# GpSimd's elementwise work handed to ScalarE and VectorE in a retention + two-MLP kernel, with a planner that knows of shared access

## The chip, the core and the metric

The kernel runs on one core of a Trainium2 chip. The metric is the device time of one execution in microseconds. Engines are named as the profile names them: PE (TensorE, matmuls; PEld its weight loads), DVE (VectorE), ACT (ScalarE), POOL (GpSimd), SP (SyncE, which issues the DMAs).

## The reference

Retention attention (scores times a decay mask, no softmax) gives 2304 tokens of 512 features. Two MLPs follow.

```python
scores = (q @ k^T) / sqrt(64); x = (scores * D) @ v        # 4 batches, 8 heads, 576 x 64
h = max(x @ w_in, 0);  x = (h * h) @ w_out                 # 512 -> 2048 -> 512
g = x @ w_gate;  out = (g * sigmoid(g) * (x @ w_val)) @ w_out2   # 512 -> 1536 -> 512
```

## The kernel before, in words

**Matmuls in three parts.** Every fp32 operand of the MLPs is split into a rounded high part, `hi`, a ScalarE copy, and a low part, `lo`, a VectorE subtraction (helper `split`, L283, and others like it). A product is then three matmuls: high x high, high x low, low x high (`three`, L200 to L202; in `o_piece` L1217 to L1219).

**The first MLP** works through five blocks of tokens. The first two multiply plainly. The last three, some 210 to 464 us, use seven products in place of eight on 2x2 blocks (`mlp1_s`, once for each of 8 pairs of feature blocks, so 24 times). This needs sums of quarters of x, T1 to T4 (`fetch_x1`: two on VectorE, two on GpSimd), and of the weights, S1 to S4 (GpSimd, L326). For each half, `finish` squares the activation on GpSimd (L852), rounds it on ScalarE and takes the low part on VectorE (L864). The weights of the second MLP are rounded to float32, split and stored meanwhile (`convert2_pair`, with four sums on GpSimd, L405).

**The second MLP** makes three passes of 768 tokens. A pass has 12 steps, one for each block of 128 features. Each step (`mlp2_gv`) runs seven products of six 384-column matmuls into two PSUM banks, MA and MB by turns; between them stand pieces of the output product (`o_piece`, three 256-column matmuls, L1217 to L1219). VectorE adds the products up: C11 (L1078, behind product 2), C22 (L1081, into the tile `m`, behind product 5), C12 (L1084, behind 6), and t1 and t2 (L1097, L1100, times the value half). ScalarE copies products out (L1069, `m` and `u`) and takes the sigmoid (L1090); VectorE multiplies it in (L1094). Product 7 goes into the bank that C22 frees, product 4 into the one that C11 frees.

Two steps make a pair. The activations of a pair give four sums (S3, S1, S2, S4: `act_sum`, GpSimd, L1156), and these and the four blocks themselves are split into operands (`operand`, tiles `at`). At the end of a pass a tail of output pieces runs (products P1 to P7 of the output). In it ScalarE and VectorE add up the passes' results (`sums_out`: copies L1258, additions from PSUM L1265) with two sums of 128x768 on GpSimd (`both`, L1271). In the same time the next pass's x is made: seven x parts (B11, B12 ... T4) are split into `xc`, and T1 to T4 are four subtractions of 128x768 on GpSimd (`fetch_x`, L967). A part's `xc` tile comes free when the last step of the pass before has used it.

**The order** on every engine is made by a planner (`Plan.emit`). Each operation has an engine, a duration in us, dependencies and a rank. The planner plays the program through: of the operations that can start first it takes the one with the lowest rank (the sums behind a product have -3, activations and operands -2, x parts 4 to 60, weight conversions 100 and more), emits it, and moves on. Each engine then runs its list in that order and waits in place. In the planner of before, engines don't disturb each other.

Of the kernel before, what the change touches and what calls it, by code (L numbers as in the profile page):

```python
# [64 lines left out]
class Op:  # L65


    __slots__ = ("eng", "us", "fn", "deps", "after", "rank", "kb", "n", "out", "left", "ready", "end", "fill")

    def __init__(self, eng, us, fn, deps, after, rank, kb):  # L70
        self.eng, self.us, self.fn, self.rank, self.kb = eng, us, fn, rank, kb
        self.deps, self.after = list(deps), list(after)
        self.out, self.left, self.ready, self.end, self.fill = [], 0, 0.0, None, None


class Plan:
# [10 lines left out]
    def __call__(self, eng, us, fn, deps=(), rank=0.0, kb=0, key=None, after=()):  # L87


        o = Op(eng, us, fn, deps, after, rank, kb)  # L90
        o.n = len(self.ops)
        self.ops.append(o)
        if key is not None:
            self.named[key] = o
        return o

    def emit(self):
# [10 lines left out]
        free, lanes, left = {}, 0.0, len(self.ops)  # L108
        while left:
# [48 lines left out]
def kernel(ctx: ExitStack, tc: tile.TileContext, units, qtab, tab, w1, w2, out):  # L158
# [75 lines left out]
    def round32(box, rank, apart=False):  # L234
# [36 lines left out]
        p4 = do("DVE", 1.34, d4, [p2, p3, o2], rank)  # L271
# [3 lines left out]
    def split(get, n, out, place, rank, deps, cols=None):  # L275
# [10 lines left out]
        return do("DVE", 0.16 + 0.53 * n / 512, lo, [h], rank)  # L286
# [26 lines left out]
    def convert_s(p, rank):  # L313
# [16 lines left out]
        x = do("POOL", 0.87, add(2, 3, 2, ALU.add), [ld], rank)  # L330
        x = do("POOL", 0.87, add(3, 0, 3, ALU.subtract), [x], rank)
        x = do("POOL", 0.87, add(0, 2, 0, ALU.subtract), [x], rank)
        x = do("POOL", 0.87, add(1, 1, 0, ALU.subtract), [x], rank)
# [14 lines left out]
    def convert2_pair(box, f, rank, plain, summed, steps):  # L348
# [38 lines left out]
        front = lambda: do("DVE", 0.69, lo(low, 0, n), [h, *low_free], rank)  # L387
        back = lambda: do("DVE", 0.43, lo(rest, n, 768), [h], rank)
# [13 lines left out]
        for o, x, y, op in steps:  # L402
            def add(o=o, x=x, y=y, op=op):
                w = st["fm"].rearrange("p (s n) -> p s n", s=4)
                nc.gpsimd.tensor_tensor(out=w[:, o], in0=w[:, x], in1=w[:, y], op=op)  # L405
            l = do("POOL", 0.87, add, [l if o != steps[0][0] else need[o], need[o]], rank)
        h = do("ACT", 1.03, hi2, [l], rank)
        l = do("DVE", 1.22, lo2, [h], rank)
# [98 lines left out]
    def att_prep(c, rank):  # L507
# [148 lines left out]
    def mlp1_act(j, f):  # L656
# [138 lines left out]
    def mlp1_s(j, p, pieces):  # L795
# [93 lines left out]
        r0 = do("ACT", act, relu("g0", hi_half), [c12], -2)  # L889
# [4 lines left out]
        c21 = name("s21", do("ACT", act, relu("g1", lo_half, "MA"), [N_op[j, p, 6]], -3))  # L894
        hlo_op[j, f1] = finish("g1", f1, lo_half, [c21, e1])
# [54 lines left out]
    def fetch_x(b, rank):  # L950
# [15 lines left out]
        def sub(o, a, c):  # L966
            return lambda: nc.gpsimd.tensor_tensor(out=at(o), in0=at(a), in1=at(c), op=ALU.subtract)  # L967
# [18 lines left out]
        parts_in_order(part, lambda *a, deps: do("POOL", 2.4, sub(*a), deps, min(rank, 4) if b else rank), ld)  # L986
# [60 lines left out]
    def mlp2_gv(s, pieces):  # L1047
# [77 lines left out]
        si1 = name("si1", do("DVE", dve, silu(0, lo_half), [sg], -2))  # L1125
# [13 lines left out]
        si2 = name("si2", do("DVE", dve, silu(1, hi_half), [sg], -2))  # L1139
        t2_ = name("t2", do("DVE", dve, t2, [si2, c22_], -2))  # L1140
# [10 lines left out]
    def act_sum(b, q, out, x, y, op, deps, rank=-2):  # L1151
        def go():
# [415 lines left out]
```

## Time and profile before

| | us |
|---|---|
| median of 3 runs (888.36 to 889.59) | 888.45 |
| the profiled execution | 887.93 |
| its span, first to last instruction | 886.1 |
| PE busy | 865.6 |
| DVE busy | 639.2 |
| ACT busy | 471.6 |
| POOL busy | 354.5 |

A matmul's end is modelled and overlaps the next one's start, so PE's pace is read from the distance of starts. An instruction on DVE that waits stands later in its timeline; what it waited for is in brackets, where the trace shows it.

### The profile page before, as it was taken

How to read it: one execution, taken by the hardware profiler on the slowest of the kernel's cores; microseconds unless marked ns; L12 is line 12 of the kernel's file. 1: busy time of each engine (PE TensorE's matmuls, PEld its weight loads, DVE VectorE, ACT ScalarE, POOL GpSimd, SP SyncE). 2: the span in 40 equal slices, each digit the busy share in tenths (PEclk: the TensorE clock that was granted, in tenths of full speed). 3: DMA queues.
4: the chain of work that ended last, by engine and by line, in shares of the span. 5: the costliest groups of instructions: out<-in, count | busy, mean ns of one | idle time of the engine just before them, and what ended most of it. 6: DMA issues, size and time to landing. Idle time of an engine off the chain costs nothing.

```text
span 886.1 us, 15973 instructions
## 1 busy us (share of the span) xinstructions
PE 865.6 (98%) x5995; PEld 809.3 (91%) x5995; DVE 639.2 (72%) x938; ACT 471.6 (53%) x898; POOL 354.5 (40%) x333
## 2 busy tenths in 40 slices
PE   9799999999999999999999999989999989999998
PEld 7688878999899899989999999989999989999998
DVE  4899895637878978897887878596555587555565
ACT  2767674347667667676564544463333354333353
POOL 4131205653646566556581434252122144221231
PEclk9999999999999999999999999999999999999999
DMA  9777868998989698879889998959777767775772
GB/s 359 259 272 269 313 218 258 398 375 282 367 285 352 245 344 315 289 238 341 319 311 323 301 417 317 348 196 330 273 254 259 266 206 259 262 276 214 260 261 74
DMA packets 113085, 254.84 MB, mean 288 GB/s; under 512 B 8560, under 2 KB 67696, under 8 KB 103664
## 3 DMA queue, kind: packets, MB, share of 16 engines
q1 hardware_dynamic: 113008, 253.82, 81.2%
q8 instruction: 47, 0.77, 0.3%
q14 instruction: 30, 0.25, 0.1%
HBM read 195.59 MB, written 58.20 MB: 286 GB/s over the span
## 4 chain that ended last, share of the span: by engine, by line
PE 76%; DVE 13%; issue 3%; DMA 3%; ACT 3%; POOL 2%; SPq 0%; ACTq 0%; POOLq 0%; DVEq 0%
PE gv L200 12%; PE gv L201 12%; PE gv L202 12%; PE acc L201 6%; PE acc L202 6%; PE acc L200 6%; DVE at L283 4%; PE acc L1219 3%; PE acc L1217 3%; PE acc L1218 3%; PE hps L200 3%; PE hps L202 2%; PE hps L201 2%; PE sc L528 1%; PE xs L568 1%
## 5 line engine op out<-in xcount | busy, mean ns | idle before, releaser
L200 PE MATMUL gv<-xc,w 128*128 128x384 f32 x504 | 171.6, 340 | 6.5 <-DVE m L1081 5.7
L201 PE MATMUL gv<-xc,w 128*128 128x384 f32 x504 | 170.3, 338 | 0.0
L202 PE MATMUL gv<-xc,w 128*128 128x384 f32 x504 | 170.0, 337 | 0.0
L201 PE MATMUL acc<-h,w 128*128 128x512 f32 (+1 forms) x320 | 117.8, 368 | 1.1 <-DVE h L679 0.8
L202 PE MATMUL acc<-h,w 128*128 128x512 f32 (+1 forms) x320 | 117.6, 368 | 0.2
L852 POOL TENSOR_TENSOR g<-g 128x256 f32<-128x256 f32 x96 | 86.8, 913 | 77.2 <-ACT g L848 76.5
L200 PE MATMUL acc<-h,w 128*128 128x512 f32 (+1 forms) x320 | 117.3, 367 | 0.0
L200 PEld LDWEIGHTS gv<-xc,w 128*128 128x128 f32 x504 | 94.9, 188 | 9.2 <-DVE m L1081 7.0
L201 PEld LDWEIGHTS gv<-xc,w 128*128 128x128 f32 x504 | 95.3, 189 | 0.2
L202 PEld LDWEIGHTS gv<-xc,w 128*128 128x128 f32 x504 | 95.0, 189 | 0.0
L1219 PE MATMUL acc<-w,at 128*128 128x256 f32 x288 | 81.6, 283 | 0.0
L1218 PE MATMUL acc<-w,at 128*128 128x256 f32 x288 | 81.3, 282 | 0.0
L1217 PE MATMUL acc<-w,at 128*128 128x256 f32 x288 | 81.2, 282 | 0.0
L1069 ACT COPY m<-gv 128x384 f32<-128x384 f32 x72 | 34.6, 481 | 83.1 <-PE gv L202 81.9
L1156 POOL TENSOR_TENSOR st<-g,rs 128x384 f32<-128x384 f32 x18 | 21.7, 1204 | 141.1 <-DVE rs L1100 141.1
L405 POOL TENSOR_TENSOR f<-f 128x256 f32<-128x256 f32 x72 | 66.2, 919 | 29.2 <-DVE cw L362 18.4
L202 PEld LDWEIGHTS acc<-h,w 128*128 128x128 f32 x320 | 60.1, 188 | 10.9 <-DVE w L283 1.0
L864 DVE TENSOR_TENSOR h<-g,h 128x256 fp32r<-128x256 f32 x96 | 62.6, 652 | 7.6 <-ACT h L860 7.5
L200 PE MATMUL gv<-xb,w 128*128 128x256 f32 x238 | 67.2, 282 | 0.8 <-ACT m L835 0.4
L201 PEld LDWEIGHTS acc<-h,w 128*128 128x128 f32 x320 | 60.1, 188 | 8.6 <-DVE h L679 1.3
L201 PE MATMUL gv<-xb,w 128*128 128x256 f32 x238 | 66.9, 281 | 0.1
L202 PE MATMUL gv<-xb,w 128*128 128x256 f32 x238 | 66.8, 281 | 0.0
(175 smaller groups left out, 2246.4 us busy)
## 6 DMA issues: line engine op xcount, KB each, us to landing
w<-wdS SPq DMA_DIRECT2D x36, 1024.0 KB, 5.6
raw<-w SPq DMA_DIRECT2D x34, 1024.0 KB, 7.3
w<-wdP SPq DMA_DIRECT2D x36, 768.0 KB, 7.0
w<-ws SPq DMA_DIRECT2D x94, 256.0 KB, 4.9
w<-wdOP SPq DMA_DIRECT2D x54, 256.0 KB, 4.8
w<-wdOS SPq DMA_DIRECT2D x18, 768.0 KB, 7.4
ws<-cw SPq DMA_DIRECT2D x16, 512.0 KB, 7.2
wdS<-cw SPq DMA_DIRECT2D x12, 512.0 KB, 5.3
```

The lines of the kernel that those rows point to most:

```text
L200: nc.tensor.matmul(ps, lhsT=wh, rhs=xh, start=first, stop=False, skip_group_check=onto)
L201: nc.tensor.matmul(ps, lhsT=wh, rhs=xl, start=False, stop=False, skip_group_check=onto)
L202: nc.tensor.matmul(ps, lhsT=wl, rhs=xh, start=False, stop=last, skip_group_check=onto)
L283: nc.vector.tensor_tensor(out=t[:, 1], in0=get(), in1=t[:, 0].bitcast(F32), op=ALU.subtract)
L405: nc.gpsimd.tensor_tensor(out=w[:, o], in0=w[:, x], in1=w[:, y], op=op)
L852: return lambda: nc.gpsimd.tensor_tensor(out=st[key][:, half], in0=st[key][:, half], in1=st[key][:, half], op=ALU.mult)
L864: nc.vector.tensor_tensor(out=t[:, 1, half], in0=st[key][:, half], in1=t[:, 0, half].bitcast(F32), op=ALU.subtract)
L1069: nc.scalar.copy(out=st[name], in_=late[bank][:, :HALF])
L1156: nc.gpsimd.tensor_tensor(out=o, in0=i, in1=k, op=op)
L1217: nc.tensor.matmul(ps, lhsT=ah, rhs=wh, start=product not in ONTO and q == 0 and off == 0, stop=False, skip_group_check=True)
L1218: nc.tensor.matmul(ps, lhsT=ah, rhs=wl, start=False, stop=False, skip_group_check=True)
L1219: nc.tensor.matmul(ps, lhsT=al, rhs=wh, start=False, stop=q == NQ - 1, skip_group_check=True)
```

## The change

Five groups of operations leave GpSimd: the 96 squares of the first MLP go to ScalarE (`Square`); the x subtractions of both MLPs (6 and 12), the two sums at each pass's end (6) and the sums of activations (72) go to VectorE. GpSimd keeps the attention's scalings and the sums of weights (L326, L405).

The planner gets a new rule. Operations with `lock=True`, and all of GpSimd's, run at a share of their speed while one of the other engine's runs beside them: VectorE at 0.5, GpSimd at 0.62. The durations that the planner is given are lowered to match. All orders are then made anew.

```diff
+SHARE = {"DVE": 0.5, "POOL": 0.62}
...
             free[o.eng] = t + o.us
+            if o.lock:
+                other = run.get("POOL" if o.eng == "DVE" else "DVE")
+                us = o.us
+                if other and other[0].end > t + 1e-9:
+                    x, since, both, left_x = other
+                    left_x -= max(0.0, min(t, both) - since) * SHARE[x.eng] + max(0.0, t - max(both, since))
+                    first = min(us / SHARE[o.eng], left_x / SHARE[x.eng])
+                    ends = [t + first + max(0.0, w - first * SHARE[e]) for w, e in ((us, o.eng), (left_x, x.eng))]
+                    grow(x, ends[1])
+                    run[x.eng] = x, t, t + first, left_x
+                    run[o.eng] = o, t, t + first, us
+                    free[o.eng] = ends[0]
+                else:
+                    run[o.eng] = o, t, t, us
...
-        p1 = do("DVE", 1.0 if apart else 0.8, d1, [o1], rank)
-        p2 = do("DVE", 1.0 if apart else 0.8, d2, [p1], rank)
-        p3 = do("DVE", 0.87, d3, [o2] if apart else [p2, o2], rank)
+        p1 = do("DVE", 0.69, d1, [o1], rank, lock=True)
+        p2 = do("DVE", 0.69, d2, [p1], rank, lock=True)
+        p3 = do("DVE", 0.75, d3, [o2] if apart else [p2, o2], rank, lock=True)
...
         def sub(o, a, c, deps):
-            eng, us = ("DVE", 0.69) if o in ("T1", "T2") else ("POOL", 1.5)
-            e = nc.vector if eng == "DVE" else nc.gpsimd
-            return do(eng, us, lambda: e.tensor_tensor(out=at(o), in0=at(a), in1=at(c), op=ALU.subtract), deps, rank)
+            eng, us = ("DVE", 0.69)
+            return do(eng, us, lambda: nc.vector.tensor_tensor(out=at(o), in0=at(a), in1=at(c), op=ALU.subtract), deps, rank, lock=True)
...
         def square(key, half):
-            return lambda: nc.gpsimd.tensor_tensor(out=st[key][:, half], in0=st[key][:, half], in1=st[key][:, half], op=ALU.mult)
+            return lambda: nc.scalar.activation(out=st[key][:, half], in_=st[key][:, half], func=ACTF.Square)
+
+        def gate(key, half, deps, bank=None):
+            r = do("ACT", act, relu(key, half, bank), deps, -3 if bank else -2)
+            return r, do("ACT", act, square(key, half), [r], -2)
...
-            r = do("POOL", 0.87, square(key, half), deps, -2)
-            h = do("ACT", act, hi, [r, y_op.get(order1[i - 2])], -2)
-            return do("DVE", 0.58, lo, [h], -2)
+            h = do("ACT", act, hi, [*deps, y_op.get(order1[i - 2])], -2)
+            return do("DVE", 0.42, lo, [h], -2, lock=True)
...
-        def sub(o, a, c):
-            return lambda: nc.gpsimd.tensor_tensor(out=at(o), in0=at(a), in1=at(c), op=ALU.subtract)
+        def sub(o, a, c, deps):
+            eng, us = ("DVE", 0.96)
+            return do(eng, us, lambda: nc.vector.tensor_tensor(out=at(o), in0=at(a), in1=at(c), op=ALU.subtract), deps, min(rank, 4) if b else rank, lock=True)
...
-            nc.gpsimd.tensor_tensor(out=o, in0=i, in1=k, op=op)
-
-        s_op[b, q, out] = do("POOL", 1.18, go, deps, rank)
+            e.tensor_tensor(out=o, in0=i, in1=k, op=op)
+
+        eng, us, e = ("DVE", 0.55, nc.vector) if out in ("S3","S1","S2","S4") else ("POOL", 1.02, nc.gpsimd)
+        s_op[b, q, out] = do(eng, us, go, deps, rank, lock=True)
...
-                nc.gpsimd.tensor_tensor(out=box(dst), in0=box(dst), in1=box(src), op=ALU.add)
-            c_op[b, name] = do("POOL", 2.9, go, deps, -3)
+                nc.vector.tensor_tensor(out=box(dst), in0=box(dst), in1=box(src), op=ALU.add)
+            c_op[b, name] = do("DVE", 0.96, go, deps, -3, lock=True)
```

What this does to the order: on PE every matmul keeps its place. VectorE has 96 instructions more, ScalarE 96 more, GpSimd 192 fewer. Lines of the changed kernel stand up to 27 lower in the file than the same ones of before.

VectorE, last step of pass 1, before: `rs<-gv` is C11, `m<-gv` is C22, `at` are operand splits and `xc` splits of the next pass's x.

```order
L1078 TENSOR_TENSOR rs<-gv_2049,m_6299 128x384
L283 TENSOR_TENSOR xc<-ys,xc 128x768
L283 TENSOR_TENSOR at<-st,at 128x384
L283 TENSOR_TENSOR at<-rs,at 128x384 x4
L1081 TENSOR_TENSOR m_6344<-gv_2048,m_6344 128x384
L1084 TENSOR_TENSOR rs<-gv_2049,u_6329 128x384
L1094 TENSOR_TENSOR rs<-rs,sg 128x384
L283 TENSOR_TENSOR xc<-ys,xc 128x768
```

The same place after the change:

```order
L1104 TENSOR_TENSOR rs<-gv_2049,m_6299 128x384
L305 TENSOR_TENSOR at<-st,at 128x384
L305 TENSOR_TENSOR at<-rs,at 128x384 x4
L1120 TENSOR_TENSOR rs<-rs,sg 128x384
L1107 TENSOR_TENSOR m_6346<-gv_2048,m_6346 128x384
L305 TENSOR_TENSOR xc<-ys,xc 128x768
L1110 TENSOR_TENSOR rs<-gv_2049,u_6328 128x384
L1123 TENSOR_TENSOR rs<-gv_2048,rs 128x384
L305 TENSOR_TENSOR xc<-ys,xc 128x768
```

Ahead of C22 the x split is gone (it follows C22), and the product with the sigmoid, `rs<-rs,sg`, has moved up.

VectorE, end of the tail of pass 1, before: `oc` from `gv_2050` and `hps` is the addition behind output product P6.

```order
L283 TENSOR_TENSOR xc<-ys,xc 128x768
L283 TENSOR_TENSOR at<-rs,at 128x384 x2
L283 TENSOR_TENSOR xc<-ys,xc 128x768
L283 TENSOR_TENSOR at<-rs,at 128x384
L283 TENSOR_TENSOR xc<-ys,xc 128x768
L283 TENSOR_TENSOR at<-rs,at 128x384 x2
L1265 TENSOR_TENSOR oc<-gv_2050,oc 128x512
L1265 TENSOR_TENSOR oc<-hps,oc 128x256
L283 TENSOR_TENSOR at<-rs,at 128x384
L283 TENSOR_TENSOR xc<-ys,xc 128x768
L283 TENSOR_TENSOR at<-rs,at 128x384
```

The same place after:

```order
L993 TENSOR_TENSOR ys<-ys 128x2x384
L305 TENSOR_TENSOR at<-rs,at 128x384 x2
L993 TENSOR_TENSOR ys<-ys 128x2x384
L305 TENSOR_TENSOR at<-rs,at 128x384
L1292 TENSOR_TENSOR oc<-gv_2050,oc 128x512
L1292 TENSOR_TENSOR oc<-hps,oc 128x256
L1298 TENSOR_TENSOR oc<-oc 128x768 x2
L1292 TENSOR_TENSOR oc<-acc_5444,oc 128x512
L1292 TENSOR_TENSOR oc<-hps,oc 128x256
L305 TENSOR_TENSOR at<-rs,at 128x384 x2
L305 TENSOR_TENSOR xc<-ys,xc 128x768 x2
L993 TENSOR_TENSOR ys<-ys 128x2x384
```

Between the splits stand three of the four subtractions (`ys<-ys`; the first is a few rows above), and the two pass-end sums (`oc<-oc`) follow the first addition, the second addition follows them; two x splits and the last subtraction come behind. In the next row C11 of pass 2 follows.

ScalarE, where the third of the first MLP's five blocks turns into the fourth, before: `g<-g` is the activation's Relu, `h<-g` its rounding, `m<-hps` a product copied out of PSUM, `f<-raw` a conversion of the second MLP's weights, `yt<-acc` the third block's result.

```order
L848 ACTIVATE g_3307<-g_3307 128x256
L848 ACTIVATE g_3253<-g_3253 128x256
L860 CAST h<-g_3253 128x256
L241 ACTIVATE f<-raw 128x1024
L919 COPY yt<-acc 128x512
L848 ACTIVATE g_3307<-gv_2048 128x256
L860 CAST h<-g_3253 128x256
L835 COPY m_3360<-hps 128x256
```

A like place after; here the second `g<-g` of a tile is its square:

```order
L869 ACTIVATE g_3247<-g_3247 128x256
L856 COPY m_3276<-gv_2049 128x256
L885 CAST h<-g_3175 128x256
L873 ACTIVATE g_3247<-g_3247 128x256
L400 CAST cw<-f 128x1024
L869 ACTIVATE g_3298<-g_3298 128x256
L873 ACTIVATE g_3298<-g_3298 128x256
L263 ACTIVATE f<-raw 128x1024
L885 CAST h<-g_3247 128x256
L869 ACTIVATE g_3298<-gv_2048 128x256
```

The squares stand in ScalarE's list between the Relu and the rounding.

## Rows read from the trace of the kernel before

**Rows 1.** The page, part 1: engine, busy us (share of the span), instructions.
```profile
PE 865.6 (98%) x5995; PEld 809.3 (91%) x5995; DVE 639.2 (72%) x938; ACT 471.6 (53%) x898; POOL 354.5 (40%) x333
```

**Rows 2.** Busy us by stretch: PE, PEld, DVE, ACT, POOL; granted clock; DMA share; GB/s.
```profile
200.00:460.00 260.00, 258.01 (x1680) 234.63 (x1679) 217.62 (x314) 175.28 (x369) 156.76 (x166) 1.00 0.87 306
```

**Rows 3.** Waits of PE in the whole span: us in total, times, longest.
```profile
PE gv L200 <- DVE m L1081: 5.7, 3, 2.8
PE hps L201 <- DVE x L600: 1.8, 1, 1.8
...
PE hps L1217 <- DVE oc L1265: 1.1, 2, 0.6
PE acc L201 <- DVE h L679: 0.8, 1, 0.8
...
PE gv L200 <- ACT m L835: 0.4, 1, 0.4
...
PE hps L200 <- DVE g L842: 0.2, 1, 0.2
```

**Rows 4.** Timeline of PE at the end of pass 1: start, us, engine, line, operation.
```profile
578.18 0.33 PE L201 MATMUL gv<-xc,w 128*128 128x384 f32 x1
578.36 0.34 PE L202 MATMUL gv<-xc,w 128*128 128x384 f32 x1
581.46 0.69 PE L200 MATMUL gv<-xc,w 128*128 128x384 f32 x1 [2.76 <-DVE m L1081]
581.94 0.52 PE L201 MATMUL gv<-xc,w 128*128 128x384 f32 x1
```

**Rows 5.** Busy us by stretch, columns as in Rows 2.
```profile
28.00:31.00 3.00, 1.63 (x7) 1.35 (x8) 2.45 (x3) 0.52 (x1) 0.15 (x1) 1.00 0.52 130
...
581.40:584.80 3.40, 3.35 (x13) 3.35 (x14) 2.36 (x4) 0.90 (x2) 0.00 (x0) 0.53 0.42 138
```

**Rows 6.** Timeline of DVE in the same place.
```profile
573.87 0.56 DVE L1078 TENSOR_TENSOR rs<-gv,m 128x384 f32<-128x384 f32 x1 [1.50 <-PE gv L202]
...
575.67 5.26 DVE L283 TENSOR_TENSOR at<-rs,at 128x384 fp32r<-128x384 f32 x4
580.85 0.55 DVE L1081 TENSOR_TENSOR m<-gv,m 128x384 f32<-128x384 f32 x1
581.32 0.54 DVE L1084 TENSOR_TENSOR rs<-gv,u 128x384 f32<-128x384 f32 x1
```

**Rows 7.** Timeline of POOL in the same place.
```profile
575.37 4.21 POOL L967 TENSOR_TENSOR ys<-ys 128x768 f32<-128x768 f32 x2 [2.13 <-DVE xc L283]
```

**Rows 8.** Groups by line and shape: count | busy us, mean ns | idle before.
```profile
L852 POOL TENSOR_TENSOR g<-g 128x256 f32<-128x256 f32 x96 | 86.8, 913 | 77.2 <-ACT g L848 76.5 <-DMA wdS<-f 0.3
...
L246 ACT ACTIVATE r<-raw 128x1024 int32<-128x1024 uint16 x34 | 39.0, 1148 | 0.0
...
L669 ACT ACTIVATE r<-r 128x256 f32<-128x256 f32 x16 | 6.7, 419 | 0.5
...
L733 DVE TENSOR_TENSOR xs<-xs 128x512 f32<-128x512 f32 x6 | 4.8, 807 | 0.1
```

**Rows 9.** Timeline of DVE in a quiet block of pass 2.
```profile
662.93 0.56 DVE L1100 TENSOR_TENSOR rs<-m,rs 128x384 f32<-128x384 f32 x1
665.44 0.56 DVE L1078 TENSOR_TENSOR g<-gv,m 128x384 f32<-128x384 f32 x1 [1.95 <-PE gv L202]
```

**Rows 10.** Timeline of DVE in the tail of pass 1.
```profile
586.68 0.55 DVE L1100 TENSOR_TENSOR rs<-m,rs 128x384 f32<-128x384 f32 x1
...
598.88 0.95 DVE L283 TENSOR_TENSOR xc<-ys,xc 128x768 fp32r<-128x768 f32 x1
599.74 0.55 DVE L283 TENSOR_TENSOR at<-rs,at 128x384 fp32r<-128x384 f32 x1
...
602.02 0.68 DVE L1265 TENSOR_TENSOR oc<-gv,oc 128x512 f32<-128x512 f32 x1
```

**Rows 11.** Timeline of PE, the first matmul of pass 2.
```profile
606.77 0.34 PE L200 MATMUL gv<-xc,w 128*128 128x384 f32 x1
```

More of the change, by code (lines that the diff above doesn't have):

```diff
@@ L65, with __init__ @@
 class Op:
-    __slots__ = ("eng", "us", "fn", "deps", "after", "rank", "kb", "n", "out", "left", "ready", "end", "fill")
-    def __init__(self, eng, us, fn, deps, after, rank, kb):
+    __slots__ = ("eng", "us", "fn", "deps", "after", "rank", "kb", "n", "out", "left", "ready", "end", "fill", "lock")
+    def __init__(self, eng, us, fn, deps, after, rank, kb, lock):
         self.eng, self.us, self.fn, self.rank, self.kb = eng, us, fn, rank, kb
         self.deps, self.after = list(deps), list(after)
-        self.out, self.left, self.ready, self.end, self.fill = [], 0, 0.0, None, None
+        self.out, self.left, self.ready, self.end, self.fill, self.lock = [], 0, 0.0, None, None, lock or eng == "POOL"
 class Plan:
@@ L85, in __init__, with __call__ @@
         self.ops, self.named = [], {}
-    def __call__(self, eng, us, fn, deps=(), rank=0.0, kb=0, key=None, after=()):
-        o = Op(eng, us, fn, deps, after, rank, kb)
+    def __call__(self, eng, us, fn, deps=(), rank=0.0, kb=0, key=None, after=(), lock=False):
+        o = Op(eng, us, fn, deps, after, rank, kb, lock)
         o.n = len(self.ops)
@@ L107, in emit, with grow @@
                 waiting.setdefault(o.eng, []).append(o)
-        free, lanes, left = {}, 0.0, len(self.ops)
+        free, lanes, left, run = {}, 0.0, len(self.ops), {}
+        def grow(o, end):
+            for x, whole in o.out:
+                if whole:
+                    x.ready = max(x.ready, x.ready if x.end else end + (0.0 if x.eng == o.eng else 0.08))
+            o.end = free[o.eng] = end
         while left:
@@ L132, in emit @@
             else:
-                o.end = t + o.us
+                o.end = free[o.eng]
             for x, whole in o.out:
@@ L270, in round32 @@
         converts.append(o1)
-        p4 = do("DVE", 1.34, d4, [p2, p3, o2], rank)
+        p4 = do("DVE", 1.24, d4, [p2, p3, o2], rank)
         r_users.append(p4)
@@ L329, in convert_s @@
         ld = do("SP", 0.4, load, [wf_saved[p], f_users[-2]], rank - 20, kb=512, after=raw_loads[-1:])
[L330 to L333, printed above, removed]
+        x = do("POOL", 0.75, add(2, 3, 2, ALU.add), [ld], rank)
+        x = do("POOL", 0.75, add(3, 0, 3, ALU.subtract), [x], rank)
+        x = do("POOL", 0.75, add(0, 2, 0, ALU.subtract), [x], rank)
+        x = do("POOL", 0.75, add(1, 1, 0, ALU.subtract), [x], rank)
         def store():
@@ L386, in convert2_pair @@
                     [("xbdone", NB - 1), ("ysv", NB - 2)] if home == "xs" else [("ysv", NB - 1)])
-        front = lambda: do("DVE", 0.69, lo(low, 0, n), [h, *low_free], rank)
-        back = lambda: do("DVE", 0.43, lo(rest, n, 768), [h], rank)
+        front = lambda: do("DVE", 0.69, lo(low, 0, n), [h, *low_free], rank, lock=True)
+        back = lambda: do("DVE", 0.43, lo(rest, n, 768), [h], rank, lock=True)
         if steps is GV_SUMS:
@@ L405, in add @@
                 nc.gpsimd.tensor_tensor(out=w[:, o], in0=w[:, x], in1=w[:, y], op=op)
[L406 removed]
+            l = do("POOL", 0.75, add, [l if o != steps[0][0] else need[o], need[o]], rank)
         h = do("ACT", 1.03, hi2, [l], rank)
[L408 removed]
+        l = do("DVE", 1.22, lo2, [h], rank, lock=True)
         e = w_dram[summed, f]
@@ L518, in att_prep @@
         if c not in FIRST:
-            qs_op[c] = do("POOL", 1.45, qs, [A_op[c], Q_op[c]], rank, after=[ks_op[c - 1]])
+            qs_op[c] = do("POOL", 1.27, qs, [A_op[c], Q_op[c]], rank, after=[ks_op[c - 1]])
         if c not in LAST:
-            ks_op[c] = do("POOL", 1.25, ks, [V_op[c], tab_op], rank, after=[qs_op[c]])
+            ks_op[c] = do("POOL", 1.04, ks, [V_op[c], tab_op], rank, after=[qs_op[c]])
     def att_scores(c, rank, fill=None):
@@ L893, in mlp1_s @@
         product(6, "MA", [c22])
-        c21 = name("s21", do("ACT", act, relu("g1", lo_half, "MA"), [N_op[j, p, 6]], -3))
-        hlo_op[j, f1] = finish("g1", f1, lo_half, [c21, e1])
+        c21, r1 = gate("g1", lo_half, [N_op[j, p, 6]], "MA")
+        name("s21", c21)
+        hlo_op[j, f1] = finish("g1", f1, lo_half, [r1, e1])
         y(take_y[3])
@@ L984, in part @@
             return l
-        parts_in_order(part, lambda *a, deps: do("POOL", 2.4, sub(*a), deps, min(rank, 4) if b else rank), ld)
+        parts_in_order(part, sub, ld)
         do.named["ysdone", b] = x_chain[-1]
@@ L1138, in mlp2_gv @@
         sg = do("ACT", act, sig(1, hi_half), [c12_, sg], -2)
-        si2 = name("si2", do("DVE", dve, silu(1, hi_half), [sg], -2))
-        t2_ = name("t2", do("DVE", dve, t2, [si2, c22_], -2))
+        si2 = name("si2", do("DVE", dve, silu(1, hi_half), [sg], -2, lock=True))
+        t2_ = name("t2", do("DVE", dve, t2, [si2, c22_], -2, lock=True))
         other(2)
```

12 lines of the change are left out of this document (6 added, 6 removed).

## The prediction

> **What bounds the kernel now.** I read first the page's engine line, then the waits of PE, then the stretch around the longest wait on each engine. PE is busy 865.6 of 886.1 us [rows 1]: 20.5 us is all that can be won, unless matmuls themselves slow down. The order shows every matmul at its old place, so only waits change.
>
> The table of waits tells whose they are [rows 3]. The largest entry is 5.7 us in three waits, two of about 2.8 us, where product 7 of a step waits for `m` (the sum C22, L1081). They lie in the last step of pass 1 and of pass 2. At pass 1's end the matmul before the gap starts at 578.36 and the next at 581.46, where its neighbours stand 0.18 apart [rows 4]. Behind the gap one lasts 0.52 instead of 0.33, and the granted clock of 581.4 to 584.8 is 0.53, nearly all of it at the 1.2 GHz level [rows 5]. So the price of one such place is 2.8 us of idleness and 3.4 x (1 - 0.53) = 1.6 us of slow matmuls: 4.4.
>
> VectorE's timeline says why C22 was late [rows 6]. Its instructions are 0.47 apart when nothing disturbs them (580.85 to 581.32), but the four operand splits that stand ahead of C22 take 5.26 us, 1.3 each. In just that time GpSimd runs two subtractions, 575.37 to 579.58 [rows 7]. I read this as two engines slowing each other on SBUF.
>
> **The change part by part.** The profiled execution took 887.93 us (886.1 of span and 1.8 around it), 0.5 under the median 888.45; I sum against 887.93.
>
> *x subtractions and the last step of a pass.* In the new order five splits and one product (`rs<-rs,sg`) stand ahead of C22, and no GpSimd instruction is left there. From the start of C11 at 573.87 the seven take 7 x 0.47 = 3.3, to 577.2. C22 also needs product 5, whose last matmul was six intervals before the one at 578.36, at 577.3, and lasts 0.34: 577.65. C22 then starts near 577.8, ends 0.56 later, and product 7, free at 578.36 + 0.18, waits 0 to 0.2. Both places: 2 x 4.4 = 8.8 us gone. Bounds: 0 if the splits stay slow, 9.0 at most.
>
> *What takes the place of the stall: the tail of a pass.* The subtractions, the pass-end sums and three sums of activations now stand among the splits on VectorE. From the last activation product of pass 1 to C11 of pass 2 the order has 14 splits and 3 sums of activations at 0.47, 3 x-splits, 4 subtractions and 2 pass-end sums of 768 elements at 0.86 (598.88 to 599.74), and four additions from PSUM, two at 0.60 (the 0.68 of the first less the 0.08 by which neighbours overlap) and two of half the size at an estimated 0.33 [rows 10]: 8.0 + 7.7 + 1.9 = 17.6 us. A subtraction is priced as an x-split, which reads two tensors of that size in SBUF. The time between those two points is some 22 us, from 586.68 [rows 10] to a C11 two products (12 x 0.175) behind 606.77 [rows 11]. But the first addition needs P6 of the last pair, 15 output pieces ahead of the pass's end. A piece is three matmuls of 256 columns at two thirds of 0.175 each, 0.35 us, so P6 is done 5.3 us before pass 2 begins. Behind it stand 0.9 + 1.7 + 0.9 + 0.9 + 1.7 + 0.9 = 7.0 us, up to C11 at +1.7; C11 is due at +2.2. The margin is half a microsecond, and 0.7 more before product 4 waits. I take 0 here, bounds 0 to 2 us a pass end. The wait of 1.1 us on `oc` (L1265) in these tails [rows 3] goes, since that addition no longer stands behind slowed splits: +1.1, bounds 0 and 1.1.
>
> *Sums of activations.* 72 leave GpSimd. On VectorE each costs about 0.47. In an odd step three of them come between the last product (662.93) and the next C11 (665.44), where VectorE is idle 1.95 us [rows 9]: 1.4 fits, with 0.5 left. Cost 0; if that cover failed by 0.2 in each of the 18 pairs, 3.6 us.
>
> *Squares.* 96 squares leave GpSimd (0.91 each) for ScalarE, where a square of 128x256 takes 0.419 [rows 8]: 40.2 us more. In the stretch of the three seven-product blocks ScalarE is busy 175.3 of 260 us [rows 2], so 215.5, or 83%. PE waited for it there 0.4 us in one entry [rows 3]. I cost it at 0; the cover is the slack of the copies of `m` and `u`, and its loss is the slow rival below. The activation's chain gets shorter: 0.42 on the engine that makes the next step anyway, in place of 0.91 and a hop.
>
> *First MLP's x subtractions.* Six more on VectorE at 0.81 [rows 8] is 4.9 us, beside 217.6 busy of 260 [rows 2]. GpSimd loses 96 squares there, which gives VectorE far more than it takes. Of the seven smaller waits behind the first 200 us, from 0.8 to 0.2 and 2.6 together [rows 3], I take half: +1.3, bounds -1 and 2.6.
>
> *First 200 us.* Nothing moves engine, but the planner's new costs reorder rounding on VectorE; PE waits there up to 1.8 at once [rows 3]. I take 0, bounds -3 and +2.
>
> *Sum.* 8.8 + 1.1 + 1.3 = 11.2 off, less 1.2 for new small waits (an estimate between 0 and the 3.6 above): 10 off. 887.93 - 10 = 877.9; I give 878.
>
> **Rivals.**
> - *VectorE becomes the tail's bound* (0.17). For it: the margin at C11 is half a microsecond. Each 0.1 us that the instructions of the last stretch or the chain behind P6 run over is then paid at two pass starts. A C11 or x-split that comes 2 us too late, twice, gives 4 us back: 882. If the clock falls as behind the 2.8 us gaps, it is 2 x (2 + 1.6) = 7, and 885, which I take as its price. In the trace the clock stayed at 1.00 around the wait of 1.8 us for `x` near 28 us [rows 3, 5], which speaks for the smaller figure. The Trainium skill (TensorE: Matmul & The Clock Gate, Part 1) calls the throttled state the default, which only activity releases; by it the new pauses would cost the clock too, and the larger figure would hold. Against the rival: 17.6 us of work stand in 22.
> - *The relief does not come* (0.08): splits are slow for another reason, such as waits for ScalarE's casts. Then C22 again starts at 573.9 + 0.5 + 5 x 1.3 + 0.5 = 581.4, and both stalls stay: 887 to 888, no change. Against it: GpSimd's two subtractions cover exactly the slow splits.
> - *ScalarE holds up PE in the first MLP* (0.15), the slower side. ScalarE runs in order, and a conversion's activation takes 1.15 us [rows 8]; at 83% a copy of `m` can find one ahead of it and a square too, 1.6 us. It decides once a copy ends later than one product and two output pieces after its own product, about 2 us. If each of 24 pairs loses 0.8 us, that is 19, and with the 10 won, 897. Against it: 0.4 us waited so far.
>
> **How the numbers follow.** My forecast has 0.60, and its own range is 874 to 882. The rivals have 0.17, 0.08 and 0.15. The range 873.5 to 889.5 takes in the first two and the beginning of the third; some 0.05 lies below and 0.12 above. Under 0.2% (1.8 us) this kernel can't tell a change from none. Faster is 0.60 + 0.17 = 0.77, the same 0.08, slower 0.15.
>
> **What would show it.** The waits of PE should have no entry of 2.8 us on C22, the granted clock should stay at 1.00 around the pass ends, and splits there should stand 0.47 apart. New waits of PE at the start of passes 2 and 3, on `xc` or C11, would show the first rival; waits on `m` or `u` copies from 200 to 460 us the third. I am wrong if the stalls at the pass ends stay, or if what PE gains there it loses in the first MLP.

## The result and the profile after

The changed kernel takes 876.25 us (median of 4 runs, 875.07 to 877.39), against 888.4 for the one before on the same chip (4 runs, 886.47 to 889.59): a ratio of 0.9865, 95% interval 0.9842 to 0.9888. The prediction was 878. The profiled execution took 875.07 us, the shortest of the four, with a span of 873.1, 13.0 shorter than before; by the medians it is 12.2.

The page's engine line after, columns as in [rows 1]:

```profile
PE 859.2 (98%) x5995; PEld 807.5 (92%) x5995; DVE 625.5 (72%) x1034; ACT 505.3 (58%) x994; POOL 132.3 (15%) x141
```

VectorE has 96 instructions more and is busy 13.7 us less: what it took over costs less than what it no longer waits for.

PE's waits after, columns as in [rows 3]:

```profile
PE hps L224 <- DVE w L305: 2.0, 1, 2.0
PE hps L223 <- DVE x L622: 1.6, 1, 1.6
PE spare L577 <- DVE P L559: 1.5, 1, 1.5
...
PE hps L584 <- POOL kv L533: 0.4, 1, 0.4
```

The 5.7 us on `m` that led [rows 3] have no successor. The three that lead now lie in the first 200 us. Behind 200 us three waits of 0.4 to 0.6 us are left, two of them in the last tail.

VectorE in the last step of pass 1, the place of [rows 6]:

```profile
569.72 0.56 DVE L1104 TENSOR_TENSOR rs<-gv,m 128x384 f32<-128x384 f32 x1 [0.91 <-PE gv L224]
570.19 0.55 DVE L305 TENSOR_TENSOR at<-st,at 128x384 fp32r<-128x384 f32 x1
570.66 1.96 DVE L305 TENSOR_TENSOR at<-rs,at 128x384 fp32r<-128x384 f32 x4
572.53 0.55 DVE L1120 TENSOR_TENSOR rs<-rs,sg 128x384 f32<-128x384 f32 x1
573.61 0.56 DVE L1107 TENSOR_TENSOR m<-gv,m 128x384 f32<-128x384 f32 x1 [0.52 <-ACT xc L301]
574.08 0.95 DVE L305 TENSOR_TENSOR xc<-ys,xc 128x768 fp32r<-128x768 f32 x1
```

The four splits take 1.96 us where they took 5.26. C22 (L1107) starts 3.9 us behind C11, where it was 7.0, and VectorE is idle 0.52 ahead of it: it is early enough. (The row names ScalarE's cast as what ended this wait. The last matmul of product 5, which C22 needs, starts at 573.16 and lasts 0.34, so it ends within 0.04 us of that cast.) Two stretches after, columns as in [rows 2] and [rows 5]; the second holds the place of the old stall, and its clock is 1.00:

```profile
200.00:460.00 260.00, 260.00 (x1707) 238.64 (x1706) 193.25 (x328) 211.77 (x471) 54.96 (x64) 1.00 0.91 311
570.00:585.00 15.00, 15.00 (x113) 15.00 (x112) 13.82 (x26) 10.25 (x22) 0.00 (x0) 1.00 0.93 300
```

Since the 5995 matmuls stand in one order in both kernels, each start can be subtracted from its counterpart. That gives where the time went; the stretches go by the time of before:

```
stretch (us of before)             after less before
0 to 200    attention, weights          +1.26
200 to 575  first MLP, pass 1           -5.41  (-4.00 of it by 450)
575 to 600  stall of pass 1             -4.45
600 to 700  (0.80 at an addition oc)    -0.93
700 to 725  stall of pass 2             -4.52
725 to 850  (0.86 at an addition oc)    -0.73
850 to end  last tail                   +1.72
sum                                    -13.06
```

The last tail loses where the others gain. VectorE there, after:

```profile
860.34 2.02 DVE L1298 TENSOR_TENSOR oc<-oc 128x768 f32<-128x768 f32 x2
...
863.40 1.02 DVE L305 TENSOR_TENSOR at<-rs,at 128x384 fp32r<-128x384 f32 x2
```

And PE:

```profile
864.00 0.39 PE L1246 MATMUL acc<-w,at 128*128 128x256 f32 x1 [0.57 <-DVE at L305]
865.73 0.39 PE L1244 MATMUL acc<-w,at 128*128 128x256 f32 x1 [0.52 <-DVE oc L1292]
```

The two pass-end sums now run on VectorE, ahead of the last two operand splits, and PE waits for these; before, the sums ran on GpSimd beside them.

### The profile page after: what moved, and what is told of

Read it like the earlier page. It is cut to its first block, busy times and chain, and to the rows that moved or that the text cites. A ratio compares the mean times of both kernels' runs of the same rounds, so it can differ in the third digit from the quotient of the medians.

```text
span 873.1 us, 15883 instructions
## 1 busy us (share of the span) xinstructions
PE 859.2 (98%) x5995; PEld 807.5 (92%) x5995; DVE 625.5 (72%) x1034; ACT 505.3 (58%) x994; POOL 132.3 (15%) x141
## 4 chain that ended last, share of the span: by engine, by line
PE 91%; DVE 4%; ACT 2%; DMA 1%; issue 1%; POOL 1%; DVEq 0%; ACTq 0%; POOLq 0%
PE gv L222 13%; PE gv L223 13%; PE gv L224 13%; PE acc L224 7%; PE acc L223 7%; PE acc L222 7%; PE acc L1246 4%; PE acc L1244 4%; PE acc L1245 4%; PE hps L222 4%; PE hps L224 4%; PE hps L223 3%; PE sc L550 1%; PE xs L590 1%; PE xs L577 1%; PE hps L1355 1%
## 5 line engine op out<-in xcount | busy, mean ns | idle before, releaser
L427 POOL TENSOR_TENSOR f<-f 128x256 f32<-128x256 f32 x72 | 62.0, 860 | 273.9 <-DVE cw L384 141.9
L224 PEld LDWEIGHTS acc<-h,w 128*128 128x128 f32 x320 | 60.1, 188 | 10.9 <-DVE w L305 1.0
L223 PEld LDWEIGHTS acc<-h,w 128*128 128x128 f32 x320 | 60.1, 188 | 6.4
L222 PEld LDWEIGHTS acc<-h,w 128*128 128x128 f32 x320 | 60.1, 188 | 6.3
L889 DVE TENSOR_TENSOR h<-g,h 128x256 fp32r<-128x256 f32 x96 | 45.4, 472 | 20.9 <-ACT h L885 20.0
L1107 DVE TENSOR_TENSOR m<-gv,m 128x384 f32<-128x384 f32 x36 | 20.1, 558 | 52.9 <-PE gv L224 50.1
```

Of the source, the lines that this page charges most:

```text
L222: nc.tensor.matmul(ps, lhsT=wh, rhs=xh, start=first, stop=False, skip_group_check=onto)
L223: nc.tensor.matmul(ps, lhsT=wh, rhs=xl, start=False, stop=False, skip_group_check=onto)
L224: nc.tensor.matmul(ps, lhsT=wl, rhs=xh, start=False, stop=last, skip_group_check=onto)
L889: nc.vector.tensor_tensor(out=t[:, 1, half], in0=st[key][:, half], in1=t[:, 0, half].bitcast(F32), op=ALU.subtract)
L1107: nc.vector.tensor_tensor(out=st["m5"], in0=late["MA"][:, :HALF], in1=st["m5"], op=ALU.add)
```

## The experiments

All ratios are to the kernel before on the same chip. Theory A is the prediction's: GpSimd's subtractions slow VectorE's splits, and that makes C22 late.

**e1, the suspect taken away.** Before, with eight of GpSimd's subtractions left out (those of passes 2 and 3); the order of the rest stays.

```diff
-parts_in_order(part, lambda *a, deps: do("POOL", 2.4, sub(*a), deps, ...), ld)
+parts_in_order(part, lambda *a, deps: do("POOL", 2.4, (lambda: None) if b else sub(*a), deps, ...), ld)
```

> Kernel before, same order on every engine, but the x subtractions of passes 2 and 3 of the second MLP (8 instructions on GpSimd) are left out, so that its products use wrong x parts. Theory A (GpSimd's subtractions slow the splits that run beside them): both waits of 2.8 us on C22 at the pass ends go, with the slow clock behind them, and the splits there stand 0.47 apart; 8 to 10 us faster than before, 878 to 880. Rival B (the splits wait for ScalarE's casts or are simply too many ahead of C22): the waits stay at over 2 us each, 886 to 888.

878.2 us (876.99 to 880.48), ratio 0.9894 (0.9871 to 0.9916). VectorE in the last step of pass 1:

```profile
574.96 0.95 DVE L283 TENSOR_TENSOR xc<-ys,xc 128x768 fp32r<-128x768 f32 x1
...
576.29 2.08 DVE L283 TENSOR_TENSOR at<-rs,at 128x384 fp32r<-128x384 f32 x4
578.30 0.56 DVE L1081 TENSOR_TENSOR m<-gv,m 128x384 f32<-128x384 f32 x1
```

In the old order, with the x split still ahead of C22, the splits take 2.08 us, and the stall is gone. Behind 230 us the distance to before's starts changes by more than 0.3 us only at the two pass ends, by some 5.4 us each (the additions `oc` with them). GpSimd's subtractions are the cause. How they do it stands in the kernel before, where the row of four splits [rows 6] is made of unlike ones. Of VectorE, the first two:

```profile
575.67 2.22 DVE L283 TENSOR_TENSOR at<-rs,at 128x384 fp32r<-128x384 f32 x1
...
577.81 2.18 DVE L283 TENSOR_TENSOR at<-rs,at 128x384 fp32r<-128x384 f32 x1
```

Each begins 0.3 us behind the start of one of GpSimd's subtractions (575.37 to 577.47 and 577.55 to 579.58) and ends 0.4 behind that one's end. The other two splits take 0.55 each, and they begin when GpSimd is done.

**e6, the suspect put back.** After, with the second MLP's twelve subtractions on GpSimd.

```diff
-            eng, us = ("DVE", 0.96)
-            return do(eng, us, lambda: nc.vector.tensor_tensor(out=at(o), ...
+            eng, us = ("POOL", 2.04)
+            return do(eng, us, lambda: nc.gpsimd.tensor_tensor(out=at(o), ...
```

> The changed kernel with the second MLP's twelve x subtractions on GpSimd again; the order of VectorE's other work in the last step of each pass is the same. Theory A (the two 4.4 us places of the kernel before came from GpSimd's subtractions slowing VectorE's splits ahead of C22): both stalls are back, 2.5 to 3 us of wait and about 1.5 us of slow clock each, 883 to 886 us, and the splits ahead of C22 stand over 1 us apart. Rival B (it was VectorE's order, where an x split stood ahead of C22, or the planner's rule, that removed the stall): 875 to 878 us, no wait on C22.

884.42 us (879.34 to 887.04), ratio 0.9957 (0.9938 to 0.9977). The time is theory A's, the place is not. GpSimd:

```profile
579.75 4.38 POOL L993 TENSOR_TENSOR ys<-ys 128x768 f32<-128x768 f32 x2 [42.90 <-DVE xc L305]
588.84 4.17 POOL L993 TENSOR_TENSOR ys<-ys 128x768 f32<-128x768 f32 x2 [4.71 <-DMA w<-wdOP]
```

VectorE in the same place:

```profile
578.25 0.56 DVE L1107 TENSOR_TENSOR m<-gv,m 128x384 f32<-128x384 f32 x1 [0.52 <-ACT xc L301]
578.72 0.95 DVE L305 TENSOR_TENSOR xc<-ys,xc 128x768 fp32r<-128x768 f32 x1
...
589.20 2.09 DVE L1182 TENSOR_TENSOR st<-st,g 128x384 f32<-128x384 f32 x1
591.33 2.10 DVE L1182 TENSOR_TENSOR rs<-rs,st 128x384 f32<-128x384 f32 x1
...
596.47 0.69 DVE L1292 TENSOR_TENSOR oc<-gv,oc 128x512 f32<-128x512 f32 x1 [1.64 <-PE gv L1246]
...
597.53 2.02 DVE L1298 TENSOR_TENSOR oc<-oc 128x768 f32<-128x768 f32 x2
```

The x split that releases GpSimd now stands behind C22, so C22 is on time and what follows is slow: two sums of activations take 2.1 us each instead of 0.56, each the length of the GpSimd instruction beside it. PE then waits for splits of the tail:

```profile
600.08 0.47 PE L1246 MATMUL acc<-w,at 128*128 128x256 f32 x1 [1.97 <-DVE at L305]
...
737.98 0.39 PE L1246 MATMUL acc<-w,at 128*128 128x256 f32 x1 [1.97 <-DVE at L305]
```

These splits are late by their place in VectorE's list, and not by the slow sums. VectorE is idle for 1.64 us ahead of the first addition, which needs product P6, and P6 is no later than everything else since 575 us (4.6 behind after). The planner put seven operand splits behind that addition, three of them right behind the pass-end sums (597.53), where after has two in all. Whether it did so because of GpSimd's subtractions isn't shown. So rival B is right about C22, and the time falls into theory A's range for another reason: e6 is no second proof of theory A. The stall of before needed both, the overlap and the order. The two equal waits also cost differently. The stretches behind them, columns as in [rows 2]:

```profile
600.00:603.40 3.40, 3.33 (x16) 3.33 (x17) 3.13 (x8) 1.34 (x2) 0.00 (x0) 0.53 1.01 346
...
738.00:741.40 3.40, 3.40 (x28) 3.40 (x29) 3.40 (x8) 1.24 (x2) 0.00 (x0) 1.00 1.02 337
```

Behind the first the clock was nearly all at 1.2 GHz and 3.4 x 0.47 = 1.6 us more were lost; behind the second it stayed at 2.4 GHz. The first rival's two prices, 2 and 3.6 us a place, both occur: against after, the starts fall back by 3.7 and by 2.2. Of the 11.0 us that this profiled execution loses against after's, another 3.7 come in the first 200 us.

**e2, the new planner alone.** After's rule and costs, all the work left on GpSimd; each moved operation is returned like this one:

```diff
-            c_op[b, name] = do("DVE", 0.96, go, deps, -3, lock=True)
+            c_op[b, name] = do("POOL", 2.04, go, deps, -3, lock=True)
```

> The changed kernel's planner with its rule of shared access, but all five groups of work stay on GpSimd (costs there 0.75 for a square, 1.36 and 2.04 for x subtractions, 1.02 for a sum of activations, 2.04 for a pass-end sum). The new order puts C22 behind three operand and x splits of pass 1's end fewer than before. Theory M (the gain comes from the move): splits stay slow, VectorE falls behind in the tails, at most 4 us of the 12 are won, 884 to 888. Theory P (the gain comes from an order planned with the slowing in it): the waits on C22 go below 0.5 us, 877 to 881.

913.09 us (912.43 to 913.45), ratio 1.0283 (1.0265 to 1.03). The rule and the lowered costs without the moves lose 25 us; neither theory expected a loss. In the starts 26.7 us go at four places between 381 and 466 us (times of before), in the first MLP and at its end, and the last conversion that writes the tile `sx` starts at 445.0 (see e4). Theory M is right about the pass ends: C22 keeps two waits of 1.8 us, so planning alone doesn't remove the stall.

**e3, the moves without the rule.**

```diff
-SHARE = {"DVE": 0.5, "POOL": 0.62}
+SHARE = {"DVE": 1.0, "POOL": 1.0}
```

> The changed kernel with the shares set to 1.0, so that the planner again knows of no slowing, while all work is moved as in the change. Theory M: hardly anything of GpSimd is left to slow VectorE behind 520 us, so the pass ends run without waits on C22 and the time is within 2 us of the changed kernel's 876.25. Theory P: the order goes wrong again where the sums of weights still run on GpSimd and at the pass ends, 881 or more.

880.83 us (879.72 to 881.51), ratio 0.9916 (0.9895 to 0.9937): the moves, with the lowered costs, are worth some 8 of the 12 us. The time is near theory P's, the place is neither's. PE's waits:

```profile
PE hps L222 <- DVE state L632: 2.9, 5, 1.4
PE hps L584 <- POOL kv L533: 2.3, 1, 2.3
...
PE xs L577 <- POOL q L538: 1.7, 1, 1.7
```

All three lie in the first 200 us. The starts are 5.7 us behind after's by 202 and stay so, but for 0.9 between 460 and 575; the pass ends are level. There GpSimd still scales the attention's operands beside VectorE.

**e4, the squares alone put back.**

```diff
-            return lambda: nc.scalar.activation(..., func=ACTF.Square)
+            return lambda: nc.gpsimd.tensor_tensor(..., op=ALU.mult)
...
-            return r, do("ACT", act, square(key, half), [r], -2)
+            return r, do("POOL", 0.75, square(key, half), [r], -2)
```

> The changed kernel with the 96 squares of the first MLP back on GpSimd (planner cost 0.75). From 200 to 460 us ScalarE falls back from 212 to about 172 us busy, GpSimd rises to about 130 and VectorE by some 20. Theory A: the first MLP's small waits come back, 1 to 3 us, 877 to 879. Rival (the squares cost ScalarE as much as they free elsewhere, or the first MLP has cover for either): within 1 us of 876.25.

910.68 us (909.71 to 913.32), ratio 1.0261 (1.0238 to 1.0285), a clear miss. One wait in PE's table makes up 23 us:

```profile
PE gv L222 <- DMA sx<-ws: 23.0, 1, 23.0
```

The tile `sx` serves the conversions of the second MLP's weights and then the loads of sums of weights, so a late conversion delays a load. Its last write by a conversion, as the view of the tile gives it (engine, operation: ns shortest/median/longest, first and last start):

```profile
L384 DVE TENSOR_TENSOR sx<-f,cw x13: 679/685/1221, 235.5 to 455.0; 128x512 fp32r<-128x512 f32 x13
```

Its last start is 455.0 us, where after has 414.8. Was it GpSimd's load, or the rule's plan?

**e10, the same without the rule.** e4's edit and e3's together.

> The changed kernel with the squares of the first MLP on GpSimd again, as in the run before on the squares, and the planner's sharing shares set to 1.0 (no rule). Theory R (the 34 us lost with the squares on GpSimd come from the rule: with much GpSimd work in the plan it draws every conversion out and spaces the second MLP's weights too late): 882 to 887 us, no wait on the load of the second MLP's S weights, ScalarE and GpSimd busier between 200 and 400 us than with the rule. Theory G (GpSimd's squares themselves, beside VectorE's added work, hold the conversions up): 905 or more, with the same long wait near 440 us. A time between 890 and 900 would leave both with a share.

885.31 us (882.35 to 889.95), ratio 0.9988 (0.997 to 1.0007): theory R. The same row:

```profile
L384 DVE TENSOR_TENSOR sx<-f,cw x13: 676/684/1228, 235.3 to 405.2; 128x512 fp32r<-128x512 f32 x13
```

The conversions end 50 us earlier on the same engines, and between 200 and 400 us VectorE and GpSimd are busier than in e4 (163.4 and 109.3 us against 145.2 and 92.7). With much GpSimd work in the plan the rule spreads conversions, the last in rank, too thinly: by the ratios 24 us. In plans without the rule the squares cost 6 us on GpSimd (e10 against e3).

**e11, the squares alone moved.** Before, one edit:

```diff
-            r = do("POOL", 0.87, square(key, half), deps, -2)
+            r = do("ACT", act, square(key, half), deps, -2)
```

with `square` as in the change.

> The kernel before with one part of the change: the first MLP's 96 squares on ScalarE, the old planner and all else as it was. Theory S (the squares on GpSimd slowed VectorE's low parts and conversions in the first MLP and made the chain to the next products longer; moving them is worth the 4 us that the changed kernel wins between 200 and 450 us): 883 to 886 us, all of the gain between 200 and 460 us, the two stalls of 2.8 us at the pass ends as before. Rival (those 4 us come from the planner's rule or the x subtractions): 887 to 889 us. Second rival (the squares hold ScalarE up in an order that wasn't planned with the rule): 890 or more.

886.36 us (884.61 to 887.34), ratio 0.998 (0.997 to 0.999). From 200 to 450 us the starts gain 2.2 us, half of after's 4.0; the stalls at the pass ends stay. But 2.3 us go to two waits for VectorE's results at 485 and 530 us, and the stall of pass 1, a wait of 2.73 us, is followed by a granted clock of 1.00 from 580.9 to 584.3 and costs 1.4 less than before's. So the whole time says little on the squares. It is just outside theory S's range, and under the rivals'. The mean of the low parts (`h<-g,h`) falls from 652 ns to 533, and to 472 in after.

**e12, the first MLP's x subtractions put back.** After, T3 and T4 on GpSimd.

```diff
-            eng, us = ("DVE", 0.69)
+            eng, us = ("DVE", 0.69) if o in ("T1", "T2") else ("POOL", 1.36)
```

> The changed kernel with the first MLP's six x subtractions on GpSimd again (planned at 1.36 us each), the squares on ScalarE. Between 200 and 450 us the changed kernel won 4.0 us, the squares alone 2.2. Theory X (the other 1.8 come from the x subtractions): 877.5 to 878.5 us, the loss in small waits on x parts where a block of tokens begins. Rival (they come from the order of conversions and squares as a whole; six instructions of GpSimd there can be hidden): 875.5 to 877 us, no new wait over 0.5 us there. Second rival (the rule draws the conversions out again because GpSimd has more in the plan): 879 or more, with a wait on the second MLP's weights.

878.07 us (876.36 to 878.83), ratio 0.9887 (0.9866 to 0.9909). Its interval overlaps with after's, so the time alone can't tell. The starts lose 1.7 us from 200 to 300, 1.1 of it at 212 us. VectorE there:

```profile
209.59 1.22 DVE L305 TENSOR_TENSOR cw<-fs,cw 128x1024 fp32r<-128x1024 f32 x1
210.72 1.50 DVE L701 TENSOR_TENSOR h<-r,h 128x256 fp32r<-128x256 f32 x1
```

GpSimd:

```profile
209.80 2.14 POOL L755 TENSOR_TENSOR xs<-xs 128x512 f32<-128x512 f32 x1 [3.70 <-DVE xs L755]
213.70 1.35 POOL L755 TENSOR_TENSOR xs<-xs 128x512 f32<-128x512 f32 x1 [1.76 <-DVE xs L755]
```

The first of these subtractions, 1.35 us where nothing disturbs it, starts just behind a VectorE split, which still takes its usual 1.22; it takes 2.14 itself, and the next VectorE instruction 1.50 for 0.43. PE waits 0.82 us for that one, the wait on `h` of [rows 3], and not for an x part as expected. With the squares' 2.2 this makes up after's 4.0: theory X, by the starts.

**e9, ScalarE's cover.** After, with each rounding copy of the first MLP's activations in the seven-product blocks done twice; the planner isn't told.

```diff
+                nc.scalar.copy(out=Hs[j, f][:, 0, half], in_=st[key][:, half])
```

> The changed kernel with each rounding copy of the first MLP's activations in the three seven-product blocks done twice on ScalarE (96 instructions of 0.42 us more, about 39 us; the result is the same). ScalarE is then busy about 251 of the 260 us from 200 to 460. Theory C (the slack of ScalarE hides work there, and the squares cost nothing because 48 us were free): under 8 us more, 876 to 884, with small waits of the tensor engine on copies of products. Theory Q (what counts is not the sum but what stands ahead of a copy in ScalarE's list, so that the price was small only by luck): 12 to 40 us more, 888 to 916, spread over all 24 pairs.

878.78 us (877.59 to 879.39), ratio 0.9906 (0.989 to 0.9923): 2.5 us more than after by the medians, 3.6 by the ratios. The stretch, columns as in [rows 2]:

```profile
200.00:460.00 260.00, 259.17 (x1698) 236.59 (x1697) 188.76 (x324) 236.16 (x558) 55.03 (x64) 1.00 0.89 307
```

With 96 instructions more on ScalarE, busy 236.2 of 260 us, PE loses 2 us here. Theory C.

**e5, the sums of activations put back on GpSimd.**

```diff
-... ("DVE", 0.55, nc.vector) if out in ("S3","S1","S2","S4") else ("POOL", 1.02, nc.gpsimd)
+... ("DVE", 0.55, nc.vector) if out in () else ("POOL", 1.02, nc.gpsimd)
```

> The changed kernel with the second MLP's 72 sums of activations on GpSimd again (planned at 1.02 us each). Theory N (their move was free and brought nothing by itself, since VectorE's gaps take them and GpSimd had room): 875 to 878.5 us, with VectorE's splits beside them slowed to 0.6 to 0.8 us and no wait of the tensor engine over 0.6 us. Rival (GpSimd's sums slow the splits ahead of C22 and C11 enough to be seen, or stand too long in the chain to the splits): 880 to 884 us, with waits on splits or on C22 at many pairs.

877.17 us (875.91 to 879.46), ratio 0.9893 (0.9875 to 0.9912): its interval overlaps with after's. Behind 200 us the starts fall back by 0.4 in all. The operand splits slow from 552 and 554 ns (mean) to 718 and 661, and VectorE's gaps hide it.

**e7, the last tail.**

```diff
-            c_op[b, name] = do("DVE", 0.96, go, deps, -3, lock=True)
+            c_op[b, name] = do("DVE", 0.96, go, deps, 0 if last else -3, lock=True)
```

> The changed kernel with one number: in the last pass the two pass-end sums on VectorE get rank 0 in place of -3, so that the last operand splits stand ahead of them. Theory T (the tail of the last pass lost 1.4 us because the two sums, 2 us, stood ahead of the last two splits): the tensor engine's waits of 0.6 and 0.5 us near 864 to 866 us go, and the end comes 1 to 1.4 us earlier: 874.5 to 875.5 us. Rival: the sums then end later, the last additions and stores behind them come as much later, and the time stays at 876 or rises by up to 1 us.

877.55 us (874.37 to 878.19), ratio 0.9887 (0.9868 to 0.9907). VectorE:

```profile
860.69 1.02 DVE L305 TENSOR_TENSOR at<-rs,at 128x384 fp32r<-128x384 f32 x2
861.63 1.94 DVE L1298 TENSOR_TENSOR oc<-oc 128x768 f32<-128x768 f32 x2
```

The splits go first and PE's wait for them is gone; the starts gain 1.7 and lose 0.8 again to a later addition, and the end comes 0.9 earlier against the rest of the execution. In the medians that doesn't show, and 877.55 is outside theory T's range: the trace bears out the theory's cause and most of its size, the time can't tell.

**e8, e7 and old costs for the first 200 us.** e7's edit; the rounding of the first MLP's weights without the rule; the attention's scalings at their old costs.

```diff
-        p1 = do("DVE", 0.69, d1, [o1], rank, lock=True)
+        p1 = do("DVE", 0.69 if apart else 0.8, d1, [o1], rank, lock=apart)
...
-            qs_op[c] = do("POOL", 1.27, qs, ...
+            qs_op[c] = do("POOL", 1.45, qs, ...
```

> The changed kernel with two edits: the pass-end sums of the last pass at rank 0, as in the run before on them, and in the first 200 us the rounding of the first MLP's weights and the attention's scalings at the planner's old durations, the rounding without the sharing rule there. Theory F (the 1.3 us that the changed kernel is behind the one before at 200 us come from the new costs in this stage): the tensor engine reaches its first product behind 200 us 1 us earlier, and the end comes 1.9 us earlier with the last tail's 0.9: 873.5 to 875 us. Rival (the rule is what keeps this stage short, and without it rounding and scalings collide as in the run with the moves alone): 877 to 881 us, with waits on the attention's scalings.

877.55 us (877.2 to 879.67), ratio 0.9894 (0.9877 to 0.9911). Theory F falls; a wait on a scaling is back at 158 us, as in e3:

```profile
PE hps L584 <- POOL kv L533: 2.5, 1, 2.5
```

No version beats the changed kernel by more than the runs can tell.

## Why the prediction was right, and where it wasn't

*The stalls, 8.8 us.* Right in mechanism and size: 4.45 + 4.52 = 9.0, with e1 showing the cause. Two readings behind it were loose. The splits were not 1.3 us each: two paid 1.7 us each and two nothing (e1's section). And 4.4 is not a fixed price of such a place: 1.6 of it is the slow clock, which came behind both stalls of this profiled execution (0.53, and 0.52 from 721.0 to 724.4) and not behind the first stall of e11. The chance of 0.08 for "the relief does not come" was not needed.

*The additions `oc`, 1.1.* 0.80 + 0.86 = 1.66, the slower start behind each wait included.

*The tail, 0 with half a microsecond of margin.* Right, and tighter than the half microsecond said. VectorE at the end of pass 1 after, the place of [rows 10]:

```profile
592.88 2.02 DVE L1298 TENSOR_TENSOR oc<-oc 128x768 f32<-128x768 f32 x2
...
598.62 0.95 DVE L993 TENSOR_TENSOR ys<-ys 128x768 f32<-128x768 f32 x1
599.74 0.56 DVE L1104 TENSOR_TENSOR g<-gv,m 128x384 f32<-128x384 f32 x1 [0.17 <-PE gv L224]
```

C11 waits for PE by 0.17 us. A subtraction lasts 0.95 and starts 0.86 ahead of its neighbour, the price taken from the x split. The first rival did not come, but e6 shows its price when splits of these 22 us do come late.

*Sums of activations, 0.* e5: 0.4 in the starts behind 200 us.

*Squares, 0; first MLP, +1.3.* This is the term that was mis-sized: 4.0 us came by 450 and 1.4 more by 575, 5.4 for 1.3, outside the bound of 2.6. The step that failed, of size and not of mechanism, priced the small waits at the idle time that the table of waits gives, and took half. They went nearly all, and each had cost more than its entry. PE before, at one of them, which the table counts as 0.17:

```profile
291.32 0.39 PE L201 MATMUL acc<-h,w 128*128 128x512 f32 x1
291.55 0.39 PE L202 MATMUL acc<-h,w 128*128 128x512 f32 x1
292.10 0.38 PE L200 MATMUL hps<-xb,w 128*128 128x256 f32 x1 [0.17 <-DVE g L842]
292.33 0.28 PE L201 MATMUL hps<-xb,w 128*128 128x256 f32 x1
292.44 0.29 PE L202 MATMUL hps<-xb,w 128*128 128x256 f32 x1
```

The idle time counts from the modelled end, 0.39 behind a start, where the next start would have been due 0.23 behind it; and the first matmul behind a wait keeps the next 0.23 off instead of 0.12. So 0.17 in the table is 0.33 + 0.11 = 0.44 in the starts (after, these two intervals are 0.22 and 0.12). Some ten such places make up the difference. The runs split the 4.0: 2.2 from the squares (e11), 1.7 from six x subtractions (e12); the 1.4 between 450 and 575 were not tested alone. ScalarE's cover was real (e9), and rival three's price of 19 far too high. The squares, measured after:

```profile
L889 DVE TENSOR_TENSOR h<-g,h 128x256 fp32r<-128x256 f32 x96 | 45.4, 472 | 20.9 <-ACT h L885 20.0
L873 ACT ACTIVATE g<-g 128x256 f32<-128x256 f32 x96 | 39.7, 417 | 1.7
```

39.7 us, 417 ns each, against the 40.2 and 419 taken from [rows 8]; the low parts behind them went from 652 ns to 472.

*First 200 us, 0.* 1.26 lost in the profiled executions. That is not a measured cost: e5, e7, e9 and e12, which keep after's order there, stand 0.3 to 0.7 from it at 200 us, and e4 and e6, with the same order too, 2.8 and 3.7. In e6 most of the 3.7 is clock: granted 0.63 from 31.0 to 34.5 us and 0.69 from 121.0 to 124.5, behind waits that after has too, where after has 1.00 in both. But the planner's rule seems to matter there more than the prediction saw: the starts lose 5.7 us without it (e3) and 3.2 with part of it gone (e8), in each some 2 of them at the wait on a scaling, which is 0.4 us in after and 2.3 and 2.5 there. Only e3's loss is clear of the spread, and only its time is clear of after's.

*New small waits, 1.2.* 1.7, in the last tail. The prediction looked at that place only for passes 1 and 2.

The sum, 10 for 13, is short by the first MLP. The gain is the moves' (8 of 12 by medians) and the rule's (4.6); rule and lowered costs without the moves lose 25.

## What to carry to other kernels

Where a VectorE instruction with two SBUF operands takes several times its usual length, look for a GpSimd instruction of the same moment before looking at VectorE's load; moving the work over can make VectorE's sum smaller. A changed order can hide the slow instruction (C22 in e6), and it can put another one too late (the splits there), so follow the released work to the next place that is tight, and look whether the engine was idle just ahead of it before blaming what was slow. A row that merges instructions gives their mean: take it apart. A planner's cost rule is tested by itself, since here it is worth 4.6 us with one placement and costs 24 with another.

## What the runs showed of the hardware

- VectorE and GpSimd take turns rather than share. A 128x384 sum of VectorE takes 0.56 us alone and 2.1 beside a GpSimd subtraction of 2.0 (e6); a split that has begun keeps its 1.22, and GpSimd's subtraction ends 0.8 us later for it (e12). The Trainium skill (SBUF — State Buffer, "SBUF: two separate sides") says so: an exclusive lock held for the whole instruction, for a VectorE instruction with two SBUF inputs against a GpSimd one that reads SBUF. The runs agree. Two instructions of VectorE with one operand in PSUM weren't slowed: L1110 and L1123 in e6 start at 579.59 and 580.28, beside GpSimd's subtraction from 579.75 to 581.61, and take 0.55 and 0.56.
- A wait of 1.97 us of TensorE was followed by 3.4 us at a granted clock of 0.53 at one pass end and by none at the next, with the same instructions around it (e6). A wait of 2.76 at the end of pass 1 was followed by 0.53 before, and one of 2.73 in the same place by 1.00 in e11. So a stall of 2 us is priced from both ends, 2.0 and 3.6, and a longer one too.
